# Linear attention beside a shifted MLP on one core: half rows of w4 in three openings, another order of the first products, one straight program

## The chip, the cores and the metric

The kernel runs on 1 core of one Trainium2 chip. The metric is device time in microseconds (us). Below, PE is TensorE (matrix products), DVE is VectorE, ACT is ScalarE, POOL is GpSimd and SP is SyncE, which issues most transfers. PSUM is the memory that PE writes to: 8 banks, each 512 float32 wide on 128 partitions.

## What is computed

```python
def reference(A_x, A_wqkv, A_wo, B_x, B_w1, B_w2, B_w3, B_w4, gate_w):
    x = A_x                                              # (1, 2048, 640)
    g = sigmoid((x * gate_w).sum(-1, keepdims=True))
    # a: linear attention, 32 heads of 20
    q, k, v = heads(x @ wqkv)
    phi = lambda t: where(t > 0, t + 1, exp(t)) + 1e-6
    kv = einsum("bhsd,bhse->bhde", phi(k), v)
    z = einsum("bhsd->bhd", phi(k))
    a = (phi(q) @ kv / (phi(q) . z + 1e-6)) @ wo
    # b: two gelu layers with layer norms, the first one's columns shifted by 1 or 2 rows
    h = gelu(layernorm(x) @ w1)                          # (640, 640)
    x1 = x + shifted(h) @ w2
    b = x1 + gelu(layernorm(x1) @ w3) @ w4               # (640, 1728), (1728, 640)
    return g * a + (1 - g) * b
```

Inputs and output are bfloat16; sums are float32 in PSUM.

## The kernel before

The 2048 rows are 16 tiles of 128, or 4 chunks of 512. A product over 640 columns of depth is 5 blocks of 128 (`KD`), one over 1728 is 13 blocks of 128 (`KFF`) and a half block of 64.

**Order.** The program is written as items (`_Items.add`) in streams, each with dependencies. A planner (`_Items.run`, line 352) takes the next item of the stream that can start first by a simulated clock, and the engines' programs are lists in that order. `_Sched.op` derives each instruction's waits from what it reads and writes. A lag of `None` in a dependency means order alone. `bank()` and `pair()` give out PSUM banks, the one that comes free first by that clock; `bank_hold` keeps banks out of their reach.

**Emission.** `_Sched.emit` (line 300) opens an `nc.Block()`, writes each engine's list as a body of its own in it, and adds final waits: POOL waits for every transfer in, SP for every transfer out, in the order of their last use.

**First stage.** `t_x` turns a tile of x by PE (five 128 x 128 products against an identity) and DVE copies it to `xT`. `q_four` (line 916) makes queries of tiles 0 to 3 with `stream` (line 893): a step (t, k) of its list is a 512 and a 128 column product with block k of `wq`; (t, None) is `t_x(t)`. Tile 0 is turned ahead of the list. `k_first` (line 925) makes keys of tile 0 the same way with `wkg`, 512 and 130 columns: the last two are a column of ones and the gate's weights, which have a transfer of their own. `phi` then reads the pair of banks with ACT and DVE. Tiles 1 to 3 are `k_tile`; from tile 4 on, the x tile is turned by a transfer on SP ("trx") and query and key tiles alternate. Between them stand the G steps (`gr_step`), which sum keys times x over all tiles, a 512 and a 128 column product each, in a pair of banks held through the whole stage; G steps 0, 1 and 2 stand behind key tile 4.

**Last stage.** `w3_group` (c, j) makes 128 of the 1728 hidden columns for chunk c into `h2T`, which has two slots. `w3_half` makes the last 64 columns for two chunks at once into `h2h`: an even tile's rows on partitions 0 to 63, an odd tile's on 64 to 127. w4's products for a tile t take columns 128 to 640 (`w4_tile`, 13 products that end in DVE's sum into `x_tok`); columns 0 to 128 are made for a whole chunk turned (`w4_turned`, then ACT's copy and a transposing transfer to `tl`, then `turned_sum` by DVE, 9 operations). The half block of 64 has only half of the array's height. `w4_half(c)` (line 1193) makes these products for a whole chunk first, opening 5 banks that the 13 full products add to later: one turned product with partitions 64 to 127 (`first`), four mains, alternately low and high, and one turned product with partitions 0 to 63. `w4_tile` of tile 15 is cut in 384 and 128 columns, so the last chunk takes 6 banks. `w4_half(0)` stands behind `w3_half(2)`, ahead of `w3_group(1, 11)`; the other three ahead of `w4_turned(c)`. Attention tiles (`a_tile`, five products of 512, and `a_turned` for a chunk) come between w4's tiles, and `out_tiles` sends finished tiles.

Of the kernel before, what the change touches and what calls it, by code (L numbers as in the profile page):

```python
# [51 lines left out]
class _Sched:  # L52
# [247 lines left out]
    def emit(self):  # L300
        nc = self.nc
        with ExitStack() as es:
# [5 lines left out]
            for k, n in self.dma_cnt.items():  # L308
                if not k.startswith("out"):
                    self.prog["pool"].append(([("d:" + k, 16 * n)], None, None))  # L310
            last = {k: i for i, k in enumerate(self.out_order)}
            for k in sorted(last, key=last.get):
                self.prog["sp"].append(([("d:" + k, 16 * self.dma_cnt[k])], None, None))
            block = es.enter_context(nc.Block())
            engs = {"pe": ("tensor", block.tensor), "act": ("scalar", block.scalar), "dve": ("vector", block.vector),
                    "pool": ("gpsimd", block.gpsimd), "sp": ("sync", block.sync)}

            def body(name):
                prog = self.prog[name]

                def run(e):
                    for (waits, fn, sem) in prog:
                        for (sk, val) in waits:
                            e.wait_ge(sems[sk], val)
                        if fn is None:
                            continue
                        ins = fn(e)
                        if sem is not None:
                            if sem.startswith("d:"):
                                ins.then_inc(sems[sem], 16)  # L330
                            else:
                                ins.then_inc(sems[sem], 1)
                return run

            for name, (_, deco) in engs.items():
                if self.prog[name]:
                    deco(body(name))
# [95 lines left out]
def _build(nc, A_x, A_wqkv, A_wo, B_w1, B_w2, B_w3, B_w4, gate_w, out, dbg=None, stop=None):  # L433
# [491 lines left out]
    def k_first():  # L925
        stream([(0, k) for k in range(KD)], wkg, 130, k_out)
# [11 lines left out]
    for i in range(4, NT + 2):  # L938
        if i < NT:
# [4 lines left out]
        for t in range(3) if i == 4 else (i - 2,):  # L944
# [465 lines left out]
```

## Time and profile before

| | us |
|---|---|
| median of 3 runs | 261.06 (260.98 to 261.1) |
| the profiled execution | 261.21 |
| its span | 259.1 |
| PE busy | 254.9 |
| DVE busy | 158.4 |
| ACT busy | 110.8 |
| POOL busy | 97.3 |

The span is the time from the first to the last instruction of one profiled execution; the metric is a little longer. A row of a timeline has start and duration in us, engine, line of the kernel, operation, out<-in, shape and count, and in brackets how long the engine had been idle and what ended that. Neighbouring instructions of one kind are merged in one row. A row of groups has the count, the busy time and the mean in ns. A row of waits has the sum in us, how many, and the longest. A row of transfers has the count, the size, and the median time from issue to landing. The granted PE clock is full in all 40 slices.

### The profile page before, as it was taken

What the parts mean: (1) busy time and instruction counts of PE and PEld (TensorE: products, weight loads), DVE (VectorE), ACT (ScalarE), POOL (GpSimd) and SP (SyncE); (2) the same over time, 40 slices, a digit from 0 to 9 for tenths busy, and PEclk for the clock granted to TensorE, in tenths of its full rate; (3) what the DMA queues carried; (4) which work ended last, traced back from release to release, by engine and by line L of the source; (5) the groups of instructions that cost most, each with busy time, mean ns of one, the idle gap of its engine ahead of it and who ended that gap; (6) DMA issues with size and microseconds to landing.
All of it is one profiled execution on the core that took longest, in us unless ns stands there. A gap on an engine that the chain in (4) does not pass through costs nothing.

```text
span 259.1 us, 3851 instructions
## 1 busy us (share of the span) xinstructions
PE 254.9 (98%) x1427; PEld 121.8 (47%) x1427; DVE 158.4 (61%) x293; ACT 110.8 (43%) x229; POOL 97.3 (38%) x154
## 2 busy tenths in 40 slices
PE   7999999999999999999999999999999999999996
PEld 3555555544445455554444444444444444444443
DVE  2497877899954699989995303998006510048136
ACT  1496777741355857684864240015510055200100
POOL 8003996869944119659681210111002210003000
PEclk9999999999999999999999999999999999999999
DMA  6858997826528699483677513115110040010322
GB/s 196 260 79 232 180 119 191 237 49 125 101 45 108 114 374 330 86 100 65 127 122 111 108 20 23 25 25 145 28 23 0 1 123 0 0 20 0 92 53 101
DMA packets 58644, 26.78 MB, mean 103 GB/s; under 512 B 49966, under 2 KB 57215, under 8 KB 58626
## 3 DMA queue, kind: packets, MB, share of 16 engines
q1 hardware_dynamic: 57122, 22.92, 42.5%
q0 software_dynamic: 1168, 3.28, 5.3%
q10 hardware_dynamic: 336, 0.35, 0.4%
q8 instruction: 11, 0.18, 0.3%
q14 instruction: 7, 0.06, 0.1%
HBM read 12.09 MB, written 2.67 MB: 57 GB/s over the span
## 4 chain that ended last, share of the span: by engine, by line
PE 97%; DMA 1%; DVE 0%; SPq 0%; issue 0%
PE ps L622 61%; PE ps L1227 22%; PE ps L828 7%; PE ps L909 2%; DMA x_tok<-in_A_x_dram 1%; PE ps L808 1%; PE ps L1127 1%; PE ps L1205 1%; PE ps L910 0%; PE ps L991 0%; PE ps L1210 0%; PE ps L809 0%; SPq L289 0%; PE ps L633 0%; PE ps L1024 0%; DVE xT L687 0%
## 5 line engine op out<-in xcount | busy, mean ns | idle before, releaser
L622 PE MATMUL ps<-xnT,w 128*128 128x512 bf16 x360 | 81.5, 379 | 0.0
L622 PEld LDWEIGHTS ps<-xnT,w 128*128 128x128 bf16 x360 | 34.5, 98 | 39.3 <-issue 0.2
L661 DVE SCALAR_TENSOR_TENSOR x_tok<-ps,stg,abx 128x512 bf16<-128x512 f32 (+2 forms) x17 | 12.2, 717 | 60.3 <-PE ps L1227 60.2
L1227 PE MATMUL ps<-w,h2T 128*128 128x512 bf16 (+2 forms) x221 | 47.0, 366 | 0.0
L644 POOL TENSOR_SCALAR abx<-x_tok,stg 128x512 f32<-128x512 bf16 x16 | 12.4, 779 | 92.1 <-DVE x_tok L661 71.6
L644 POOL TENSOR_SCALAR xn<-x_tok,st 128x640 bf16<-128x640 bf16 x32 | 38.7, 1218 | 8.9 <-DMA xnT<-xn 8.5
L678 ACT ACTIVATE h2T<-ps 128x512 bf16<-128x512 f32 x52 | 29.9, 600 | 23.5 <-PE ps L622 23.5
L1227 PEld LDWEIGHTS ps<-w,h2T 128*128 128x128 bf16 x221 | 21.2, 98 | 24.1
L678 ACT ACTIVATE tlT<-ps 128x512 bf16<-128x512 f32 x8 | 4.8, 597 | 60.7 <-PE ps L622 49.6
L678 ACT ACTIVATE Er<-ps 128x640 bf16<-128x640 f32 (+1 forms) x35 | 22.9, 660 | 18.2 <-PE ps L622 9.7
L677 ACT ACTIVATE junk<-x_tok 128x640 bf16<-128x640 bf16 x32 | 23.6, 738 | 4.7 <-DVE x_tok L659 4.2
L678 ACT ACTIVATE hsT<-ps 128x512 bf16<-128x512 f32 (+1 forms) x32 | 18.9, 595 | 14.1 <-PE ps L622 13.8
L622 PE MATMUL ps<-w,hsT 128*128 128x512 bf16 (+1 forms) x160 | 24.0, 299 | 0.0
L622 PE MATMUL ps<-wkg,xT 128*128 128x512 bf16 (+1 forms) x150 | 22.6, 299 | 0.0
L622 PE MATMUL ps<-M_sb,pqnT 128*128 128x512 bf16 x80 | 19.7, 379 | 0.0
L622 PEld LDWEIGHTS ps<-w,hsT 128*128 128x128 bf16 x160 | 13.4, 98 | 12.5
L622 PEld LDWEIGHTS ps<-wkg,xT 128*128 128x128 bf16 x150 | 12.6, 97 | 11.8
L828 PE MATMUL ps<-pk_tok,x_tok 128*128 128x512 bf16 x80 | 17.8, 379 | 0.0
L659 DVE SCALAR_TENSOR_TENSOR x_tok<-ps,x_tok 128x640 bf16<-128x640 f32 x16 | 13.1, 821 | 7.5 <-PE ps L622 6.9
L661 DVE SCALAR_TENSOR_TENSOR abx<-ps,stg,abx 128x512 f32<-128x512 f32 x16 | 11.9, 748 | 9.1 <-PE ps L622 6.4
L652 DVE TENSOR_TENSOR qprod<-qprod,pk_tok 128x640 f32<-128x640 f32 x13 | 16.3, 1254 | 0.4
L644 DVE TENSOR_SCALAR Er<-Er 128x640 bf16<-128x640 bf16 (+1 forms) x35 | 11.6, 332 | 8.0 <-ACT Er L678 7.0
(87 smaller groups left out, 284.5 us busy)
## 6 DMA issues: line engine op xcount, KB each, us to landing
w<-in_B_w_dram SPq DMA_DIRECT2D x1, 2160.0 KB, 10.0
w<-in_B_w_dram SPq DMA_DIRECT2D x1, 2080.0 KB, 15.5
x_tok<-in_A_x_dram SPq DMA_DIRECT2D x3, 640.0 KB, 6.0
out_dram<-x_tok SPq DMA_DIRECT2D x3, 640.0 KB, 3.4
w<-in_B_w_dram POOLq DMA_DIRECT2D x8, 160.0 KB, 5.1
wkg<-in_A_wqkv_dram SPq DMA_DIRECT2D x5, 160.0 KB, 4.3
wv<-in_A_wqkv_dram POOLq DMA_DIRECT2D x1, 800.0 KB, 5.8
x_tok<-in_A_x_dram SPq DMA_DIRECT2D x4, 160.0 KB, 3.4
```

The source lines that it names most:

```text
L622: ins = e.matmul(out_ap, l, r, start=(i == 0), stop=(i == n - 1))
L644: return engf(lambda e: e.tensor_scalar(out_ap, in_ap, s1, s2, op0, op1), rd, [out_ap], cost=cost)
L652: return engf(lambda e: e.tensor_tensor(out_ap, a, b_, op), [a, b_], [out_ap], cost=cost)
L659: return dve(lambda e: e.scalar_tensor_tensor(out_ap, in0, scalar, in1, op0, op1, accum_out=accum), rd, [out_ap, accum], cost=cost + 70.0)
L661: return dve(lambda e: e.scalar_tensor_tensor(out_ap, in0, scalar, in1, op0, op1), rd, [out_ap], cost=cost)
L677: return act(lambda e: e.activation(out_ap, in_ap, func, bias=bias, scale=scale, accum_out=accum), rd, wr, cost=cost)
L678: return act(lambda e: e.activation(out_ap, in_ap, func, bias=bias, scale=scale), rd, wr, cost=cost)
L808: e.matmul(ps[:, b, :], l, x_tok[:, t, 0:512], start=(t == 0), stop=(t == NT - 1))
L828: ins = e.matmul(ps[:, b, :], l, r, start=(t0 + q_ == 0), stop=(t0 + q_ == NT - 1))
L909: e.matmul(ps[:, b, 0:512], l, w[:, k, 0:512], start=(k == 0), stop=(k == KD - 1))
L1127: ins = e.matmul(o, l, r, start=st, stop=sp)
L1227: ins = e.matmul(o, l, r, start=False, stop=(i == KFF - 1), skip_group_check=shared)
```

## The change

Four things are changed. The program is emitted straight on the engines, without a block, with a barrier at its end; POOL's final waits are gone, and SP waits for the outputs in reverse order and for those transfers in that nobody waits for. `q_four`'s order is another, `k_first` makes its five wide products first, and G steps 0 and 1 stand ahead of query tile 4. `w4_half` becomes `w4_enter`: three lists of seven units (c, i), where i = 4 is a chunk's turned bank. Entry 0 stands behind both `w3_half`, which now come after `w3_group(1, 12)`; entry 1 behind w4's tile 5; entry 2 behind tile 11 and the last `a_turned`. With that the turned products and the sums move: `w4_turned(1)` behind tile 5, `w4_turned(3)` behind tile 12, and `turned_sum` 0 to 3 behind tiles 1, 6, 12 and 13.

```diff
@@ -305,36 +305,20 @@
                 sems["c:" + e] = es.enter_context(nc.semaphore("cnt_" + e))
             for k in self.dma_cnt:
                 sems["d:" + k] = es.enter_context(nc.semaphore("dma_" + k))
-            for k, n in self.dma_cnt.items():
-                if not k.startswith("out"):
-                    self.prog["pool"].append(([("d:" + k, 16 * n)], None, None))
+            seen = {w for p in self.prog.values() for (waits, _fn, _sem) in p for w in waits}
             last = {k: i for i, k in enumerate(self.out_order)}
-            for k in sorted(last, key=last.get):
+            left = [k for k in self.dma_cnt if k not in last and ("d:" + k, 16 * self.dma_cnt[k]) not in seen]
+            for k in sorted(last, key=last.get, reverse=True) + left:
                 self.prog["sp"].append(([("d:" + k, 16 * self.dma_cnt[k])], None, None))
-            block = es.enter_context(nc.Block())
...
+            engs = {"pe": nc.tensor, "act": nc.scalar, "dve": nc.vector, "pool": nc.gpsimd, "sp": nc.sync}
+
+            for name, e in engs.items():
+                for (waits, fn, sem) in self.prog[name]:
+                    for (sk, val) in waits:
+                        e.wait_ge(sems[sk], val)
+                    if fn is not None:
+                        fn(e).then_inc(sems[sem], 16 if sem.startswith("d:") else 1)
+            nc.all_engine_barrier()
 
 
 class _Items:
@@ -914,8 +898,8 @@
                 done(t, b)
 
     def q_four():
-        order = [(0, 0), (1, None), (2, None), (1, 0), (2, 0), (0, 1), (1, 1), (2, 1), (3, None), (0, 2), (1, 2), (3, 0), (0, 3), (1, 3),
-                 (0, 4), (2, 2), (1, 4), (2, 3), (2, 4), (3, 1), (3, 2), (3, 3), (3, 4)]
+        order = [(0, 0), (1, None), (2, None), (1, 0), (0, 1), (1, 1), (2, 0), (2, 1), (3, None), (0, 2), (1, 2), (0, 3), (0, 4), (1, 3),
+                 (1, 4), (2, 2), (2, 3), (2, 4), (3, 0), (3, 1), (3, 2), (3, 3), (3, 4)]
         stream(order, wq, 128, lambda t, b: phi(b, pq_tok[:, t + 1, :]))
 
     def k_out(t, b):
@@ -923,7 +907,13 @@
         activation(junk[:, 0, :], x_tok[:, t, :], ACTF.Square, accum=st1[:, 1, t:t + 1])
 
     def k_first():
-        stream([(0, k) for k in range(KD)], wkg, 130, k_out)
+        b = pair()
+        for c0, c1, b_ in ((0, 512, b), (512, D + 2, b + 1)):
+            for k in range(KD):
+                l, r, o = xT[:, k, 0:128], wkg[:, k, c0:c1], ps[:, b_, 0:c1 - c0]
+                pe(lambda e, l=l, r=r, o=o, k=k: e.matmul(o, l, r, start=(k == 0), stop=(k == KD - 1)), [l, r], [o],
+                   cost=(c1 - c0) * 0.4167 + 2.5)
+        k_out(0, b)
 
     def addA(name, dur, fn, deps=()):
         IT.add("A", name, dur, fn, deps)
@@ -936,12 +926,15 @@
     for i in range(1, 4):
         addA(("k", i), 1.36, lambda t=i: k_tile(t))
     for i in range(4, NT + 2):
+        if i == 4:
+            for t in range(2):
+                addA(("g0", t), 0.27, lambda t=t: gr_step(t), deps=[(("k", t), 2.0)])
         if i < NT:
             addA(("q", i), 1.08, lambda t=i: q_tile(t))
             addA(("k", i), 1.36, lambda t=i: k_tile(t))
             if i % 4 == 3:
                 addA(("qr", i // 4), 1.08, lambda c=i // 4: q_turned(c))
-        for t in range(3) if i == 4 else (i - 2,):
+        for t in (i - 2,):
             addA(("g0", t), 0.27, lambda t=t: gr_step(t), deps=[(("k", t), 2.0)])
 
     IT.add("LW", ("lw1",), 0.0, load_w1, deps=[(("k", 5), 0.0)])
@@ -1190,35 +1183,48 @@
     def w4_cuts(t):
         return ((0, 384), (384, 512)) if t == NT - 1 else ((0, 512),)
 
-    def w4_half(c):
-        tag_chk("h2T", c % 2, c)
-        bs = [bank() for _ in range(5 if c < NCH - 1 else 6)]
-        w4_banks[c] = bs
-        bank_hold.update(bs)
-        mains = []
-        for i in range(4):
-            for n, (n0, n1) in enumerate(w4_cuts(4 * c + i)):
-                mains.append((ps[:, bs[i if n == 0 else 5], 0:n1 - n0], i, 128 + n0, 128 + n1))
-
-        def main(e, o, i, n0, n1):
+    ENTRIES = (((0, 4), (0, 0), (0, 1), (0, 2), (0, 3), (1, 0), (1, 1)),
+               ((1, 4), (1, 2), (1, 3), (2, 0), (2, 1), (2, 2), (2, 3)),
+               ((2, 4), (3, 4), (3, 0), (3, 1), (3, 2), (3, 3)))
+
+    def w4_enter(units):
+        mains, heads, tails = [], [], []
+        for n_, (c, i) in enumerate(units):
+            if i == 4:
+                b = bank()
+                w4_banks[c, 4] = [b]
+                bank_hold.add(b)
+                heads.append((c, b, 1 if n_ == 0 else 0))
+                tails.append((c, b, 0 if n_ == 0 else 1))
+                continue
+            tag_chk("h2T", c % 2, c) if c == units[0][0] else None
+            bs = w4_banks[c, i] = [bank() for _ in w4_cuts(4 * c + i)]
+            bank_hold.update(bs)
+            for b, (n0, n1) in zip(bs, w4_cuts(4 * c + i)):
+                mains.append((ps[:, b, 0:n1 - n0], c, i, 128 + n0, 128 + n1))
+
+        def main(e, o, c, i, n0, n1):
             rows = slice(64 * (i % 2), 64 * (i % 2) + 64)
             return e.matmul(o, h2h[rows, c, 128 * (i // 2):128 * (i // 2 + 1)], w4[rows, KFF, n0:n1], start=True, stop=False)
 
-        def turned(e, par):
+        def turned(e, c, b, par, first):
             rows = slice(64 * par, 64 * par + 64)
-            o = ps[:, bs[4], :].rearrange("p (n h q) -> p n h q", h=2, q=128)[:, :, par, :]
+            o = ps[:, b, :].rearrange("p (n h q) -> p n h q", h=2, q=128)[:, :, par, :]
             return e.matmul(o, w4[rows, KFF, 0:128], h2h[rows, c, :].rearrange("p (n q) -> p n q", q=128),
-                            start=(par == 1), stop=False, skip_group_check=True)
+                            start=first, stop=False, skip_group_check=True)
 
         def fn(e):
             ins = None
             for m in mains:
                 ins = main(e, *m)
             return ins
-        rd = [h2h[:, c, :], w4[:, KFF, :]]
-        first = pe(lambda e: turned(e, 1), rd, [ps[:, bs[4], :]], cost=60.0)
-        pe(fn, rd, [m[0] for m in mains], cost=540.0)
-        pe(lambda e: turned(e, 0), rd, [ps[:, bs[4], :]], cost=110.0, after=first)
+
+        def rd(cs):
+            return [h2h[:, c, :] for c in sorted(set(cs))] + [w4[:, KFF, :]]
+        done = [pe(lambda e, h=h: turned(e, *h, True), rd([h[0]]), [ps[:, h[1], :]], cost=60.0) for h in heads]
+        pe(fn, rd([m[1] for m in mains]), [m[0] for m in mains], cost=len(mains) * 110.0)
+        for f, h in zip(done, tails):
+            pe(lambda e, h=h: turned(e, *h, False), rd([h[0]]), [ps[:, h[1], :]], cost=110.0, after=f)
 
...
@@ -1262,9 +1268,10 @@
 
     def w3_w4_half():
         w3_half(2)
-        w4_half(0)
+        w4_enter(ENTRIES[0])
 
     GEL = 1.3
+    TS_AT = {1: 0, 6: 1, 12: 2, 13: 3}
     OUT_AT = {3: 0, 7: 4, 11: 8, 13: 12, 14: 14, 15: 15}
     for c in range(NCH):
         for j in range(KD):
@@ -1312,10 +1319,10 @@
                 deps.append((("w2", NT - 1), 0.0))
             if c == 1 and 7 <= j <= 10:
                 deps.append((("a", j - 7), 0.0))
-            if c == 1 and j == KFF - 2:
+            IT.add("W3", ("w3", c, j), 1.08, lambda c=c, j=j: w3_group(c, j), deps)
+            if c == 1 and j == KFF - 1:
                 IT.add("W3", ("w3h", 0), 1.27, lambda: w3_half(0), [(("t2", u), 0.9) for u in range(4, 8)])
-                IT.add("W3", ("w3h", 2), 2.03, w3_w4_half, [(("t2", u), 0.9) for u in range(12, 16)] + [(("a", 3), 0.0), (("w4load",), 0.0)])
-            IT.add("W3", ("w3", c, j), 1.08, lambda c=c, j=j: w3_group(c, j), deps)
+                IT.add("W3", ("w3h", 2), 2.03, w3_w4_half, [(("t2", u), 0.9) for u in range(12, 16)] + [(("a", 3), 0.0), (("at", 0), 0.0), (("w4load",), 0.0)])
     for t in range(NT):
         deps = [(("zb",), 1.0), (("qr", max(t // 4, 1)), 2.0)]
         if t < 7:
@@ -1342,21 +1349,23 @@
         IT.add("AT", ("a", t), 1.08, lambda t=t: a_tile(t), deps)
         if t % 4 == 3:
             IT.add("AT", ("at", c), 1.08, lambda c=c: a_turned(c), [(("qt", t), 3.0)] + ([(("ts", c - 2), 0.0)] if c >= 2 else []))
-        deps4 = [(("a", t), 0.0), (("w3h", c - c % 2), GEL), (("w3", c, KFF - 1), GEL)]
-        if t % 4 == 0:
-            deps4.append((("w3", min(c + 1, NCH - 1), KFF - 1), 0.0))
-            if t == 0:
-                deps4.append((("a", 3), 0.0))
-                deps4.append((("w3h", 2), 0.0))
-        elif t + 3 < NT:
+        deps4 = [(("a", t), 0.0), (("w3h", 2), GEL), (("w3", c, KFF - 1), GEL), (("w3", min(c + 1, NCH - 1), KFF - 1), 0.0)]
+        if t % 4 != 0 and t + 3 < NT:
             deps4.append((("a", t + 3), 0.0))
-        if t % 4 == 0:
-            if c > 0:
-                IT.add("W4", ("w4h", c), 0.76, lambda c=c: w4_half(c), deps=deps4)
-            IT.add("W4", ("w4t", c), 2.8, lambda c=c: w4_turned(c), deps=deps4 + [(("at", c), 0.0)])
+        if t == 14:
+            deps4.append((("ts", 3), None))
+        if t == 6:
+            IT.add("W4", ("w4h", 1), 0.95, lambda: w4_enter(ENTRIES[1]), deps=deps4)
+            IT.add("W4", ("w4t", 1), 2.8, lambda: w4_turned(1), deps=[(("at", 1), 0.0)])
+        if t == 12:
+            IT.add("W4", ("w4h", 2), 0.95, lambda: w4_enter(ENTRIES[2]), deps=[(("at", 2), 0.0), (("at", 3), 0.0)])
+            IT.add("W4", ("w4t", 2), 2.8, lambda: w4_turned(2))
+        if t == 0 or t == 13:
+            IT.add("W4", ("w4t", c), 2.8, lambda c=c: w4_turned(c), deps=deps4 + [(("at", c), 0.0)] + ([(("ts", 2), None)] if c == 3 else []))
         IT.add("W4", ("w4", t), 2.8, lambda t=t: w4_tile(t), deps=deps4)
-        if t % 4 == 1:
-            IT.add("TS", ("ts", c), 0.0, lambda c=c: turned_sum(c), deps=[(("w4", t), None), (("w4t", c), 4.0), (("at", c), 4.0)])
+        if t in TS_AT:
+            u = TS_AT[t]
+            IT.add("TS", ("ts", u), 0.0, lambda u=u: turned_sum(u), deps=[(("w4", t), None), (("w4t", u), 4.0), (("at", u), 4.0)])
         if t in OUT_AT:
             IT.add("OUT", ("out", t), 0.0, lambda t=t: out_tiles(OUT_AT[t], t + 1), deps=[(("w4", t), 0.0), (("ts", c), 0.0)])
 
```

More of the change, by code (lines that the diff above doesn't have):

```diff
@@ L1232, in w4_turned @@
         tag_chk("h2T", c % 2, c)
-        b = w4_banks[c][4]
+        b = w4_banks[c, 4][0]
         w4_acc(ps[:, b, :], [(w4[:, k, 0:128], h2T[:, c % 2, k, :]) for k in range(KFF)], True)
@@ L1243, in w4_tile @@
         for n, (n0, n1) in enumerate(w4_cuts(t)):
-            b = w4_banks[c][a if n == 0 else 5]
+            b = w4_banks[c, a][n]
             o = ps[:, b, 0:n1 - n0]
```

20 lines of the change are left out of this document (removed).

## The prediction

> **What bounds the kernel now.** I read the share of busy time by engine first, then the view of what TensorE (PE) waited for, then the timeline of the stretches that the change touches.
>
> ```profile
> PE 254.9 (98%) x1427; PEld 121.8 (47%) x1427; DVE 158.4 (61%) x293; ACT 110.8 (43%) x229; POOL 97.3 (38%) x154
> ...
> PE ps L877 <- PEq L1395: 0.8, 1, 0.8
> PE ps L633 <- DMA x_tok<-in_A_x_dram: 0.5, 2, 0.3
> PE ps L909 <- DVE xT L687: 0.3, 1, 0.3
> ```
>
> PE is busy for 98% of the span, and the three rows are all the waits that the view of its waits has for the whole execution; the last two lie in the first 7 us. After that PE is an unbroken queue of products. So time is won only by waits in the head, by products that cost more than their columns, and by what lies behind the last product; what the other engines do counts only where it opens a gap.
>
> **The head: order of the first query products, K tile 0, two early G steps.**
>
> ```profile
> 5.41 0.45 PE L633 MATMUL ps<-ident,x_tok 128*128 128x128 bf16 x5 [0.32 <-DMA x_tok<-in_A_x_dram]
> 5.70 0.38 PE L909 MATMUL ps<-wq,xT 128*128 128x512 bf16 x1
> 5.90 0.49 DVE L687 COPY xT<-ps 128x640 bf16<-128x640 bf16 x1 [0.28 <-PE ps L633]
> 6.45 0.39 PE L909 MATMUL ps<-wq,xT 128*128 128x512 bf16 x1 [0.32 <-DVE xT L687]
> 6.73 0.38 PE L909 MATMUL ps<-wq,xT 128*128 128x512 bf16 x1
> ...
> 8.86 0.38 PE L909 MATMUL ps<-wq,xT 128*128 128x512 bf16 x1
> ...
> 11.57 0.38 PE L909 MATMUL ps<-wq,xT 128*128 128x512 bf16 x1
> ```
> ```profile
> 2.18 0.43 SPq L289 DMA_DIRECT2D wq<-in_A_wqkv_dram  x1
> 4.56 2.33 SPq L289 DMA_DIRECT2D wkg<-in_A_wqkv_dram  x5
> 6.93 0.43 SPq L288 DMA_DIRECT2D wkg<-in_gate_w_dram  x1
> 13.54 6.24 SPq L285 DMA_TRANSPOSE xT<-x_tok  x4
> ```
> ```profile
> wq<-in_A_wqkv_dram SPq DMA_DIRECT2D x1, 160.0 KB, 4.0
> ...
> wkg<-in_A_wqkv_dram SPq DMA_DIRECT2D x5, 160.0 KB, 4.3
> ...
> wkg<-in_gate_w_dram SPq DMA_DIRECT2D x1, 1.2 KB, 5.0
> ...
> xT<-x_tok SPq DMA_TRANSPOSE x1, 3.4
> ```
>
> The second fence is the issue of transfers on SP (start, duration), the third the time from issue to landing, the fourth number. A step (t, k) of `q_four` is a 512 and a 128 column product; from 8.86 to 11.57 lie ten steps, so one is 0.271 us. Step (2, 0), at 6.45, waits for the copy of tile 2 (5.90 + 0.49 = 6.39). The new order has (0, 1) and (1, 1) there. They need wq's block 1: issued 2.18, landed 2.18 + 4.0 = 6.18, so with the 0.06 from copy to start just seen, (0, 1) starts at 6.24. Four steps to 7.32, five transposes of tile 3 (0.29, as 5.41 to 5.70) to 7.61, fourteen steps without a wait (its tile 3 now comes last, so that its copy is hidden) to 7.61 + 14 x 0.271 = 11.40. Before, the last step ends at 11.57 + 0.27 = 11.84. Gain so far 0.44.
>
> ```profile
> 10.97 0.82 DVE L661 SCALAR_TENSOR_TENSOR pq_tok<-ps,Er 128x640 bf16<-128x640 f32 x1
> 12.02 0.38 PE L909 MATMUL ps<-wkg,xT 128*128 128x512 bf16 x1
> 13.38 4.25 PE L622 MATMUL ps<-wkg,xT 128*128 128x512 bf16 x30
> 16.43 0.82 DVE L661 SCALAR_TENSOR_TENSOR pk_tok<-ps,Er 128x640 bf16<-128x640 f32 x1
> 17.47 1.24 PE L622 MATMUL ps<-wq,xT 128*128 128x512 bf16 x5
> ```
>
> K tile 0 begins at 12.02, not 11.84: each of its steps reads 642 columns of `wkg`, the gate column too, which lands at 6.93 + 5.0 = 11.93. After the change the wide products read 512 columns only; the last block of `wkg` is issued at about 6.46 (five issues in 2.33) and lands near 10.8. So they can follow at 11.40, and the narrow ones come 1.08 later, past the gate's landing. The banks must be free too: the first pair is read until 10.97 + 0.82 = 11.79 now. Tile 0's last step moves from 9.40 (two steps behind 8.86) to 8.42 (four steps from 7.61 on), so that reading ends near 10.8. Gain 0.62 in all. The ten products of the tile are the same; wide first costs nothing by itself.
>
> K tiles 1 to 3 take 17.47 - 13.38 = 4.09, so they end at 12.76 + 4.09 = 16.85. Query tile 4 needs a transposed tile of x, on SP's own schedule: 13.54 + 3.4 = 16.94. That would eat 0.15 of the gain; the two G steps that now stand first fill it: 512 and 128 columns each, 0.54 together, to 17.39. They need `pk_tok` of tile 1, ready at 16.43 + 0.82 = 17.25 before, wanted at 17.12. VectorE's (DVE) chain runs at one tile per (16.43 - 10.97) / 5 = 1.09 and starts 0.98 sooner, so it is there near 16.3. Query tile 4 starts 0.08 sooner with 0.54 of later work done: **0.62** stays. If DVE's chain did not move, the second step would wait 0.2 and 0.42 would be left; if later transfers take it back, 0. Both ends stay for the range. Opening G's pair of banks earlier leaves three pairs for queries and keys, as later in the loop.
>
> **The half rows: three excursions for four.**
>
> ```profile
> 186.50 1.03 PE L622 MATMUL ps<-xnT,w 128*128 128x512 bf16 x4
> 187.46 0.28 PE L1210 MATMUL ps<-h2h,w 64*128 64x256 bf16 x1
> 187.46 0.71 PE L1205 MATMUL ps<-w,h2h 64*128 64x512 bf16 x4
> ...
> 188.10 0.82 PE L1227 MATMUL ps<-h2T,w 128*128 128x512 bf16 x3
> ```
>
> One record of a 512-column product is 0.38 long, products overlap: four in 1.03 start every (1.03 - 0.38) / 3 = 0.217. The last one starts at 187.15, the next full-height product was due at 187.37 and starts at 188.10: an excursion takes 0.73. Inside, half-height products start every (0.71 - 0.38) / 3 = 0.11, two at a time in the two halves of the array. Four of them and two of half that length are 0.55; 0.18 is lost in going and coming back. Four excursions are 2.92. The new three carry the same 25 products: twice six mains, 0.73 + 0.22 = 0.95, and once four with two more turned products, 0.73 + 0.11 = 0.84; 2.74 in all. Gain **0.18**, from 0 (if the wait to come back is longer with more banks open) to 0.25.
>
> Each entry now takes seven of eight banks, so the bank that was read last but one must be free.
>
> ```profile
> 150.12 0.60 ACT L678 ACTIVATE h2h<-ps 128x512 bf16<-128x512 f32 x1 [0.61 <-PE ps L1127]
> ...
> 240.87 0.75 DVE L661 SCALAR_TENSOR_TENSOR x_tok<-ps,stg,abx 128x512 bf16<-128x512 f32 x1 [1.37 <-PE ps L1227]
> 241.84 0.28 PE L1210 MATMUL ps<-h2h,w 64*128 64x256 bf16 x1
> ```
>
> Entry 0 comes right behind the two half-row products of w3 as before, only these now stand behind the last group of chunk 1. Its data and the seventh bank come from one reading, 150.12 to 150.72, and the excursion starts at 151.1 since the second half-row group hides it (0.4 to spare; 0.6 if that cover were gone). Entries 1 and 2 come behind an attention group of five products (1.08), as the fourth does now: w4's tile is read from 240.87 to 241.62, the entry starts at 241.84, 0.2 later. The eighth bank, which the attention group has just filled, is the one left out. Cost 0. Here the rule speaks against the change: the Trainium skill, TensorEngine Tiling (Array Packing), Gotcha 1: PSUM Pressure, says that row tiling raises the pressure on PSUM, with its row tiles in different banks; no row above shows a wait from it, and by it the entries would wait, which is the second rival.
>
> **The end.**
>
> ```profile
> 257.14 0.34 SPq L289 DMA_DIRECT2D out_dram<-x_tok  x1
> ...
> out_dram<-x_tok SPq DMA_DIRECT2D x1, 32.0 KB, 1.5
> ...
> SPq L302 <- PEq L302: 0.2, 1, 0.2
> ```
>
> The last transfer lands at 257.14 + 1.5 = 258.64; the span ends at 259.1, 0.46 later, with SP's other final waits, its jump and the barrier in it. The jump goes, and by waiting for the last transfer first SP finds the others done. The row of SP's exit bounds the gain at 0.2; 0 if the barrier is all of it; I take the middle, **0.1**. POOL's final waits for input transfers, which go too, were for transfers that products had used long before; they cost nothing. The Trainium skill, Advanced Engine Details and Errata, Control Flow Timing, gives about 108 ns for a compare and branch; by it alone this term would be 0.11, an estimate that no row here isolates.
>
> **Sum.** 0.62 + 0.18 + 0.10 = 0.90. The profiled execution took 261.21, so it becomes 260.31; it lies 0.15 above the median of the runs shown, 261.06, against which the forecast is 260.15.
>
> **The rivals.** (1) *The head's gain is taken back by a transfer on its own schedule.* For: SP issues x and its transposes regardless of PE. Against: PE waits for nothing behind 7 us, and the later transposes belong to tiles that PE reaches many us later. Then 260.15 + 0.62 = 260.77. (2) *The entries wait for a bank.* If DVE reads w4's tile 0.5 later, behind some other work, the 0.2 to spare becomes a wait of 0.3 at entries 1 and 2: 260.75. Against: the sums of the turned columns, DVE's longest stretches there (3.3, next fence), stand behind tiles 1, 6, 12 and 13, none right ahead of an entry.
>
> (3) *The other side: the last sum of the turned columns comes late.*
>
> ```profile
> 246.12 1.20 SPq L285 DMA_TRANSPOSE tl<-tlT  x1
> 251.78 0.68 DVE L652 TENSOR_TENSOR tlu<-tl,x_tok 128x512 f32<-128x512 bf16 x1
> 255.09 0.75 DVE L661 SCALAR_TENSOR_TENSOR x_tok<-ps,stg,abx 128x512 bf16<-128x512 f32 x1
> 256.03 1.08 DVE L661 SCALAR_TENSOR_TENSOR x_tok<-ps,stg,abx 128x384 bf16<-128x384 f32 x2 [0.19 <-PE ps L1227]
> tl<-tlT SPq DMA_TRANSPOSE x1, 2.4
> ...
> out_dram<-x_tok SPq DMA_DIRECT2D x3, 640.0 KB, 3.4
> ```
>
> Its transpose, issued 246.12, lands at 248.5, and the sum starts at 251.78: 3.3 to spare. The change puts w4's tile 12 ahead of that product, 13 x 0.217 = 2.8, and leaves 0.5. The sum lasts till 255.09, and DVE then idles 0.19 before its last tiles. So from 0.7 of lateness on, the end moves one for one. Counted from the end of chunk 2's turned product, tile 12's products end at 2.8, its reading about 0.9 later, the sum of chunk 2 at 2.8 + 0.9 + 3.3 = 7.0; only then can SP send the 640 KB of tiles 8 to 11. Chunk 3's turned product ends at 5.6, its copy takes 0.8 with the way to it, so its transpose can go at 6.4. Where SP has the output first in its queue, the transpose goes at 7.0 + 0.6 = 7.6, 1.2 late, and the end moves by 0.5; where it then waits out that transfer too, 3.4 more. Middle 2: 262.15, slower. For it: the margin shrinks to a sixth. Against: the planner issues work by when it can start, and the turned product can start at 2.8, the output at 7.0.
>
> **Chances.** Forecast 0.72, rival 1 0.08, rival 2 0.08, rival 3 0.06, and 0.06 that the planner's order elsewhere shifts and opens a gap of some tenths or more. This measurement tells about 0.2%, 0.5 us, from nothing. Faster by more: the forecast, and 0.08 from rivals 1 and 2 where they take only part: 0.80. Within: 0.11. Slower: 0.09. The range goes from all upper bounds (0.65 + 0.25 + 0.2 + a tenth of scatter: 259.85) to rivals 1 and 2: 259.85 to 260.8.
>
> **What would show it.** Right: (0, 1) near 6.24, K tile 0 near 11.4, query tile 4 near 17.4 behind two G steps, PE's view still without waits behind 7 us; three groups of half-height products, none opened by a wait on DVE; DVE's reading of the last tile, at 256.03 now, near 255.2; span near 258.2. Wrong: a releaser named ahead of the half-height products, a gap in PE between 17 and 150, the last sum of turned columns starting later than 5 us before PE's end, or more than 0.5 between the last landing and the end.

## The result, and the profile after

| | before | after |
|---|---|---|
| median of 22 runs each, one chip, us | 261.07 (260.58 to 261.58) | 260.06 (259.54 to 262.09) |
| ratio, with its 95% interval | | 0.9964 (0.9956 to 0.9972) |
| profiled execution, us | 261.21 | 260.06 |
| its span, us | 259.11 | 258.33 |
| time beyond the span, us | 2.10 | 1.73 |

The change makes the kernel 0.36% faster, about 1.0 us: more than the 0.2% that can be told. The forecast of 260.15 is 0.09 off. The table already holds something that the forecast did not have: 0.37 of the 1.15 between the two profiled executions lies outside the span.

The share of busy time, and all of what TensorE (PE) waited for, of the kernel after:

```profile
PE 254.8 (99%) x1427; PEld 122.7 (47%) x1427; DVE 158.2 (61%) x293; ACT 110.9 (43%) x229; POOL 96.8 (37%) x154
...
PE ps L861 <- PEq L1404: 0.8, 1, 0.8
PE ps L893 <- DVE xT L671: 0.3, 1, 0.3
PE ps L617 <- DMA x_tok<-in_A_x_dram: 0.2, 1, 0.2
```

As many products as before, and as before no wait behind 7 us in this view. The view has a limit: the record of a product is longer than the step to the next one, so short waits hide in it. The 0.18 that key tile 0 waited in the profile of before (11.84 to 12.02, by the prediction's own reading) is not among that kernel's waits. The starts of the products have to tell such waits. PE's busy time fell by only 0.1, although the span fell by 0.8: the sum of busy time would not have found this gain. The head, from PE's timeline:

```profile
3.77 0.71 PE L617 MATMUL ps<-ident,x_tok 128*128 128x128 bf16 x5 [0.23 <-DMA x_tok<-in_A_x_dram]
...
6.21 0.39 PE L893 MATMUL ps<-wq,xT 128*128 128x512 bf16 x1 [0.31 <-DVE xT L671]
...
6.49 0.38 PE L893 MATMUL ps<-wq,xT 128*128 128x512 bf16 x1
...
11.61 0.22 PE L894 MATMUL ps<-wq,xT 128*128 128x128 bf16 x1
11.66 1.53 PE L914 MATMUL ps<-wkg,xT 128*128 128x512 bf16 x10
...
17.11 0.38 PE L792 MATMUL ps<-x_tok,pk_tok 128*128 128x512 bf16 x1
...
17.66 1.24 PE L606 MATMUL ps<-wq,xT 128*128 128x512 bf16 x5
...
20.37 1.24 PE L606 MATMUL ps<-wq,xT 128*128 128x512 bf16 x5
```

The same view of before, query tile 5, which stands behind the same products in both kernels (queries, keys, G steps 0 to 2):

```profile
20.73 1.24 PE L622 MATMUL ps<-wq,xT 128*128 128x512 bf16 x5
```

The order is the forecast one: (1, 0) at 6.21, then (0, 1), K tile 0 right behind the last query step, two G steps, query tile 4 with no wait. Yet tile 5 comes only 0.36 sooner, and every time stands 0.25 behind the forecast: (0, 1) at 6.49 for 6.24, K tile 0 at 11.66 for 11.40, query tile 4 at 17.66 for 17.4. The first row says where it was lost. Five products of 128 columns take 0.71 here; in the profile of before the same kind took 0.45. Up to about 5.4 us PE works at half pace, and step (1, 0) is late before the new order has begun.

The three excursions, from PE's timeline:

```profile
152.89 0.92 PE L1208 MATMUL ps<-w,h2h 64*128 64x512 bf16 x6
...
193.91 1.24 PE L606 MATMUL ps<-M_sb,pqnT 128*128 128x512 bf16 x5
195.08 0.28 PE L1213 MATMUL ps<-h2h,w 64*128 64x256 bf16 x1
...
195.95 0.82 PE L1233 MATMUL ps<-h2T,w 128*128 128x512 bf16 x3
...
237.18 1.24 PE L606 MATMUL ps<-pqnT,M_sb 128*128 128x512 bf16 x5
238.36 0.28 PE L1213 MATMUL ps<-h2h,w 64*128 64x256 bf16 x2
238.48 0.59 PE L1208 MATMUL ps<-w,h2h 64*128 64x512 bf16 x5
...
239.11 0.82 PE L1233 MATMUL ps<-h2T,w 128*128 128x512 bf16 x3
```

No row names a releaser. The first, at 152.89, has its six mains right behind the half rows of w3. The second: five products from 193.91 on start every 0.215, so the next full-height product was due at 194.99; it starts at 195.95, an excursion of 0.96. The third by the same reckoning: 238.26 to 239.11, 0.85. The forecast had 0.95, 0.95 and 0.84. DVE's (VectorE's) readings that free the seventh bank:

```profile
194.11 0.75 DVE L645 SCALAR_TENSOR_TENSOR x_tok<-ps,stg,abx 128x512 bf16<-128x512 f32 x1 [1.49 <-PE ps L1233]
...
237.38 0.75 DVE L645 SCALAR_TENSOR_TENSOR x_tok<-ps,stg,abx 128x512 bf16<-128x512 f32 x1 [2.05 <-PE ps L1233]
```

They end at 194.86 and 238.13, each 0.2 before its entry, as the forecast had it. The last transfers on SP (SyncE), and DVE's last work:

```profile
248.36 1.19 SPq L285 DMA_TRANSPOSE tl<-tlT  x1
249.60 6.05 SPq L289 DMA_DIRECT2D out_dram<-x_tok  x3
...
256.57 0.34 SPq L289 DMA_DIRECT2D out_dram<-x_tok  x1
```
```profile
251.22 0.68 DVE L636 TENSOR_TENSOR tlu<-tl,x_tok 128x512 f32<-128x512 bf16 x1
...
254.53 0.74 DVE L645 SCALAR_TENSOR_TENSOR x_tok<-ps,stg,abx 128x512 bf16<-128x512 f32 x1
255.47 1.08 DVE L645 SCALAR_TENSOR_TENSOR x_tok<-ps,stg,abx 128x384 bf16<-128x384 f32 x2 [0.19 <-PE ps L1233]
```

The last transpose goes ahead of the outputs in SP's queue. With the 2.4 that it takes to land (its row, as in before) it is there at 250.76, 0.46 before the sum of the turned columns. DVE still idles 0.19 before its last two readings, so the sum does not set the end. The last output is issued at 256.57 and, with its 1.5, lands at 258.07; the span ends 0.26 later, where before it was 0.46. (At the trace's full resolution 0.29 and 0.49; below I use these.)

DVE's last reading comes at 255.47 for 256.03, 0.56 sooner: the head's 0.36 and 0.20 of the excursions, with nothing taken back between. One of the forecast's signs of being wrong was badly set: the last sum of turned columns starting later than 5 us before PE's end. It starts 4.93 before it (PE's timeline of after, then of before), but with 251.78 of before it is 4.94 there too.

```profile
247.54 8.61 PE L1233 MATMUL ps<-w,h2T 128*128 128x512 bf16 x52
```
```profile
245.30 11.42 PE L1227 MATMUL ps<-w,h2T 128*128 128x512 bf16 x65
```

So the gain of the two profiles is 0.36 in the head, 0.20 in the excursions, 0.20 at the end, and 0.37 outside the span. The head's is little more than half of its forecast, and the last was in none. The experiments ask what each part is worth by itself, why the head shows so little, and what shortens the time outside the span.

### The profile page after: what moved, and what is told of

It reads as the page before. It is cut to its first block, busy times and chain, and to the rows that moved or that the text cites. A ratio compares the mean times of both kernels' runs of the same rounds, so it can differ in the third digit from the quotient of the medians.

```text
span 258.3 us, 3824 instructions
## 1 busy us (share of the span) xinstructions
PE 254.8 (99%) x1427; PEld 122.7 (47%) x1427; DVE 158.2 (61%) x293; ACT 110.9 (43%) x229; POOL 96.8 (37%) x154
## 4 chain that ended last, share of the span: by engine, by line
PE 97%; DMA 1%; DVE 0%; issue 0%
PE ps L606 61%; PE ps L1233 22%; PE ps L812 7%; PE ps L893 2%; PE ps L792 1%; DMA x_tok<-in_A_x_dram 1%; PE ps L1120 1%; PE ps L1208 1%; PE ps L617 1%; PE ps L914 1%; PE ps L894 0%; PE ps L984 0%; PE ps L793 0%; PE ps L1213 0%; PE ps L1017 0%; DVE xT L671 0%
```

## The experiments

All kernels do the whole computation. The unchanged kernel ran beside each of the four groups, and medians and ratios are against that.

### One part at a time

The first run has the emission alone (both hunks of `emit`, with the new final waits), the second `q_four`, `k_first` and the G steps alone, the third the half rows alone; the fourth is the kernel before, unchanged. Their edits are the hunks of the diff:

```diff
-            block = es.enter_context(nc.Block())
...
+            engs = {"pe": nc.tensor, "act": nc.scalar, "dve": nc.vector, "pool": nc.gpsimd, "sp": nc.sync}
...
+            nc.all_engine_barrier()
```

> The kernel before with the new emission alone. Theory A (the prediction's sum): only the end of the span changes, 0.1 us; the time falls by 0.1, within what can be told. Theory B (two profiles: 0.46 of the span lay behind the last landing before and 0.25 after; the time less the span was 2.1 before and 1.76 after): the straight program saves about 0.2 at the end of the span and 0.35 outside it, 0.5 to 0.6 in all, and the products start and run as before.

```diff
-        stream([(0, k) for k in range(KD)], wkg, 130, k_out)
+        b = pair()
+        for c0, c1, b_ in ((0, 512, b), (512, D + 2, b + 1)):
...
+        if i == 4:
+            for t in range(2):
+                addA(("g0", t), 0.27, lambda t=t: gr_step(t), deps=[(("k", t), 2.0)])
```

> The kernel before with the head's three edits alone. Theory A: 0.62 us less. Theory B (in the changed kernel's profile the products between 3.8 and 5.4 us ran at half pace, and key tile 0 began at 11.66, not 11.40): 0.36 less whenever PE comes to full pace late, 0.6 when it comes early; so 0.35 to 0.6, and the start of the first full-pace product differs from run to run. Time less span stays 2.1 by both.

```diff
-    def w4_half(c):
...
+    def w4_enter(units):
...
-        w4_half(0)
+        w4_enter(ENTRIES[0])
```

> The kernel before with the half-row edits alone. Theory A: 0.18 us less; three groups of half-height products, 0.95, 0.95 and 0.84 long, none opened by a wait. Theory B (rival 2 of the prediction, banks): no gain or a loss, with a gap ahead of an entry that the profile names DVE for. Time less span stays 2.1 by both.

The unchanged kernel:

> The kernel before, unchanged, as a measure of what a run of it scatters in its parts: ratio 1.000 by every theory; time less span 2.1 in every run if that belongs to its program; the moment at which PE's first products reach full pace differs from its first profile if that pace depends on the run and not on the program.

Measured, against 261.13 (33 runs of the kernel before):

| kernel | median, us (11 runs) | ratio, 95% |
|---|---|---|
| emission alone | 260.93 | 0.9989 (0.998 to 0.9998) |
| head alone | 260.71 | 0.9981 (0.9973 to 0.999) |
| half rows alone | 261.04 | 0.9995 (0.9986 to 1.0003) |
| unchanged | 261.32 | 1.0005 (0.9996 to 1.0014) |

The three single gains add up to 0.35%; the whole change has 0.36%. With intervals of about 0.09% to either side, that shows only that the parts neither help nor hinder each other much. The emission alone was expected at 0.1 by the prediction's sum and at 0.5 to 0.6 by its rival; 0.11% is 0.3, between them. The half rows alone are too little for the times to tell, and the profile has to tell them. PE's timeline and DVE's last row, first of the unchanged kernel, then of the half rows alone:

```profile
77.45 1.13 PE L991 MATMUL ps<-GT,wv 128*64 128x60 bf16 x55
...
256.37 1.08 DVE L661 SCALAR_TENSOR_TENSOR x_tok<-ps,stg,abx 128x384 bf16<-128x384 f32 x2 [0.20 <-PE ps L1227]
```
```profile
77.43 1.13 PE L991 MATMUL ps<-GT,wv 128*64 128x60 bf16 x55
...
256.15 1.08 DVE L661 SCALAR_TENSOR_TENSOR x_tok<-ps,stg,abx 128x384 bf16<-128x384 f32 x2 [0.19 <-PE ps L1240]
```

From the same product in the middle to the last reading it is 178.92 unchanged and 178.72 with the half rows alone: 0.20, and the forecast was 0.18. The same stretch, at the trace's full resolution, is 178.92 in all eight profiles of this study with the old half rows and 178.71 or 178.72 in all six with the new, so one pair is enough here.

The unchanged kernel also shows what was wrong with the head. It is the same program as before, and yet its head is later. PE's timeline of this second profile of the kernel before, and then of the head alone:

```profile
3.82 0.71 PE L633 MATMUL ps<-ident,x_tok 128*128 128x128 bf16 x5 [0.27 <-DMA x_tok<-in_A_x_dram]
...
6.33 0.46 PE L909 MATMUL ps<-wq,xT 128*128 128x512 bf16 x1
6.62 0.22 PE L910 MATMUL ps<-wq,xT 128*128 128x128 bf16 x1
...
21.07 1.24 PE L622 MATMUL ps<-wq,xT 128*128 128x512 bf16 x5
```
```profile
3.77 0.72 PE L633 MATMUL ps<-ident,x_tok 128*128 128x128 bf16 x5 [0.22 <-DMA x_tok<-in_A_x_dram]
...
6.59 0.22 PE L910 MATMUL ps<-wq,xT 128*128 128x128 bf16 x1
...
20.53 1.24 PE L622 MATMUL ps<-wq,xT 128*128 128x512 bf16 x5
```

Here half pace lasts till 6.6 in both. Query tile 5 comes at 21.07 and at 20.53: 0.54 sooner. The profile of before that the forecast was made from had its full pace by 3.74 us; that of after only at 5.5. Comparing those two profiles therefore mixes the change with the pace.

### The head's three edits, one after another

The new order of `q_four` alone, and the order together with the wide products first, the G steps at their old place:

```diff
-        order = [(0, 0), (1, None), (2, None), (1, 0), (2, 0), (0, 1), (1, 1), (2, 1), (3, None), (0, 2), (1, 2), (3, 0), (0, 3), (1, 3),
-                 (0, 4), (2, 2), (1, 4), (2, 3), (2, 4), (3, 1), (3, 2), (3, 3), (3, 4)]
+        order = [(0, 0), (1, None), (2, None), (1, 0), (0, 1), (1, 1), (2, 0), (2, 1), (3, None), (0, 2), (1, 2), (0, 3), (0, 4), (1, 3),
+                 (1, 4), (2, 2), (2, 3), (2, 4), (3, 0), (3, 1), (3, 2), (3, 3), (3, 4)]
```

> The kernel before with the new order of the query products alone. Theory A (the gate column holds key tile 0, 0.18 of the head's 0.62): the queries end 0.3 to 0.45 sooner than in the kernel before at the same pace of PE, but key tile 0 still starts when the gate's transfer has landed, 11.5 to 11.95 us, with a wait in front of it; 0.1 to 0.45 gained. Theory B (the gate is not what holds it): it starts right behind the queries, with no gap, and the gain is that of the head alone, 0.5.

```diff
-        stream([(0, k) for k in range(KD)], wkg, 130, k_out)
+        b = pair()
...
+        k_out(0, b)
```

> The kernel before with the new order and the wide products of key tile 0 first, but the G steps where they were. Theory A (early G steps fill a wait for the turned x tile): query tile 4 starts with a wait when key tile 3 ends ahead of that landing, and the gain is 0.1 to 0.15 less than the head's. Theory B: the tile has landed by then (15.9 in the changed kernel's profile, 16.9 in the one before, against an end of key tile 3 at 17.1), the G steps' place costs nothing, and the gain is the head's, 0.5.

Against 261.18 (31 runs), the order alone took 261.11, ratio 1.0002 (0.9985 to 1.0018); order and wide products 260.81, 0.9984 (0.9974 to 0.9994). The first is inconclusive by its time: its runs lie between 260.36 and 262.86. PE's timeline of it, with the transfer of the gate's column (issued 6.95 on SP, the fourth number is the way to its landing):

```profile
11.63 0.22 PE L910 MATMUL ps<-wq,xT 128*128 128x128 bf16 x1
11.69 0.38 PE L909 MATMUL ps<-wkg,xT 128*128 128x512 bf16 x1
```
```profile
6.95 0.43 SPq L288 DMA_DIRECT2D wkg<-in_gate_w_dram  x1
```
```profile
wkg<-in_gate_w_dram SPq DMA_DIRECT2D x1, 1.2 KB, 4.6
```

The gate lands at 11.55, before 11.69: K tile 0 follows the queries without a gap, and the wide products first would have won nothing. PE's timeline of the second kernel, with its gate transfer:

```profile
11.89 1.53 PE L930 MATMUL ps<-wkg,xT 128*128 128x512 bf16 x10
...
17.34 1.24 PE L622 MATMUL ps<-wq,xT 128*128 128x512 bf16 x5
```
```profile
6.93 0.43 SPq L288 DMA_DIRECT2D wkg<-in_gate_w_dram  x1
```
```profile
wkg<-in_gate_w_dram SPq DMA_DIRECT2D x1, 1.2 KB, 5.1
```

Here the gate lands at 12.03 and K tile 0 starts at 11.89: without the wide products first it would have waited 0.14. Full pace begins early in this execution, as the next rows of PE's timeline show, and yet the head gains little:

```profile
3.73 0.45 PE L633 MATMUL ps<-ident,x_tok 128*128 128x128 bf16 x5 [0.18 <-DMA x_tok<-in_A_x_dram]
...
6.71 0.39 PE L909 MATMUL ps<-wq,xT 128*128 128x512 bf16 x1 [0.35 <-DMA wq<-in_A_wqkv_dram]
...
20.59 0.59 PE L622 MATMUL ps<-wq,xT 128*128 128x512 bf16 x2
```

Step (0, 1) waits here for wq's block 1, which landed at 6.66 (at the trace's full resolution; 6.19 in the profile of before, and between 5.67 and 6.66 over the 14 profiles of this study). Query tile 5, at 20.59, is only 0.14 sooner than the 20.73 of before, which had its full pace as early. So that landing moves the head as well as the pace does.

Query tile 4 stands right behind the keys without a wait although no G step fills the place: at the trace's full resolution its transposed tile of x had landed at 16.32, not 16.94. Over the 14 profiles of this study the gate's landing lies between 11.34 and 12.03, that of the transposed tile between 15.85 and 17.9.

Two of the head's three edits are insurance: they win when PE is early or a transfer late, and nothing otherwise. Of the seven profiles with the new order and at least the same dummy products, the gate lands behind the start of key tile 0 in two, by 0.14 and 0.53; early G steps filled a wait, of 0.15, in one of the six profiles that have them (the one with fewer dummy products). How much of the gain the order has by itself stays open: its one profile has the product at L991 (the one in the middle that was used above) at 76.79, 0.55 ahead of the mean of six profiles with the old head (77.34), but its ten runs show no gain, and order and wide products together 0.16%; the two intervals overlap.

### What shortens the end

The emission has two parts: no block, and other final waits. One run has the straight program with the old waits, the other the block with the new waits.

```diff
             for k, n in self.dma_cnt.items():
                 if not k.startswith("out"):
                     self.prog["pool"].append(([("d:" + k, 16 * n)], None, None))
...
-            block = es.enter_context(nc.Block())
+            engs = {"pe": nc.tensor, "act": nc.scalar, "dve": nc.vector, "pool": nc.gpsimd, "sp": nc.sync}
...
+            nc.all_engine_barrier()
```

> The kernel before, emitted straight with a barrier, but with the old final waits of POOL and SP. Theory A (the jumps are what costs): the span ends 0.3 behind the last landing, not 0.5, and time less span is 1.73 in every run, not 1.92 scattered by 0.1. Theory B (the waits are what costs): 0.5 and 1.92 as before.

```diff
-            for k, n in self.dma_cnt.items():
-                if not k.startswith("out"):
-                    self.prog["pool"].append(([("d:" + k, 16 * n)], None, None))
...
-            for k in sorted(last, key=last.get):
+            for k in sorted(last, key=last.get, reverse=True) + left:
                 self.prog["sp"].append(([("d:" + k, 16 * self.dma_cnt[k])], None, None))
...
             block = es.enter_context(nc.Block())
```

> The kernel before in its block, with the new final waits. Theory A (jumps): 0.5 from the last landing to the end of the span, time less span 1.92, as before. Theory B (waits): 0.3 and 1.73, as in the straight program.

Their times, 261.02 (0.9995, 0.9985 to 1.0004) and 261.03 (0.999, 0.9981 to 0.9999), do not tell the two apart. What does is where each loses its time. From the last landing to the end of the span at full resolution, and the mean time outside the span over the runs:

| kernel | last landing to end of span, us | outside the span, us (runs) |
|---|---|---|
| before (33 runs beside the single parts) | 0.49, 0.50 (two profiles) | 1.91 (1.68 to 2.06) |
| emission, whole | 0.29 | 1.755 (1.69 to 1.81) |
| before (31 runs beside the two below) | | 1.94 (1.68 to 2.18) |
| straight, old waits | 0.31 | 1.86 (1.82 to 1.90) |
| block, new waits | 0.43 | 1.735 (1.70 to 1.77) |
| after (22) | 0.29 | 1.73 (1.68 to 1.81) |

Inside the span most of it goes with the block: 0.18 of 0.21. The trace of before has the place: SP's branch at the block's exit starts at 258.70 and SP's next instruction at 258.88, and the straight program has no such branch. (Over the 14 profiles the first column is 0.49 or 0.50 in all six with the old emission, and 0.29 in all six straight ones with SP's new order of waits.) Outside the span most goes with the waits. Neither change alone has both.

One thing of the forecast falls here. It bounded the block's price by a row of SP's waits, 0.2 at the exit. That row is in the profile of after too, under another line, though nothing is left there to jump out of:

```profile
SPq L321 <- PEq L321: 0.2, 1, 0.2
```

The size was right by luck; the row was another thing, a wait for PE's queue; line 321 is the barrier.

Which of the waits is it? The last run has the kernel after with POOL's 45 final waits (the expectation counted 41) put back, and SP's new order kept:

```diff
+            for k, n in self.dma_cnt.items():
+                if not k.startswith("out"):
+                    self.prog["pool"].append(([("d:" + k, 16 * n)], None, None))
             seen = {w for p in self.prog.values() for (waits, _fn, _sem) in p for w in waits}
```

> The changed kernel with POOL's old final waits back (41 transfers in), SP's new order of waits kept. Theory A (POOL's waits are what lengthens the time outside the span): time less span 1.86, as in the straight program with the old waits, not 1.73; the span itself unchanged, 0.29 behind the last landing; the time 0.13 longer than the changed kernel's. Theory B (SP's order of waits is what matters): 1.73 and no difference.

It took 260.31 (6 runs), 0.9969 (0.9957 to 0.9981). Outside the span 1.895 (1.83 to 1.95), with no run in the range of after; from the last landing to the end 0.29, as after. So POOL's (GpSimd's) final waits cost about 0.17, all of it outside the span. The kernel before, beside it, had 1.88; the kernel after was not run in this group, and its 1.73 is from another. Why is open: most of these waits are for transfers that landed long before. The last is for the last transpose of turned columns, which lands at 250.97, and in the trace POOL is through with all of them by 251.17, while PE works till 256.33 and the span ends at 258.52.

### The pace of the first products

If half pace costs the head 0.3, more dummy products ahead of it could bring the full pace sooner. PE fills its wait for the first tile with them (`WARM` columns). One run takes most of them away, another adds some, also in the gaps of the list ((None, None) is 128 columns more). Only dummy products change. The kernel after runs beside them, unchanged.

```diff
-    WARM = 3072
+    WARM = 512
```

> The changed kernel with 512 columns of dummy products at the start in place of 3072, so that PE idles from 1.3 to 3.7 us. Theory B (PE comes to full pace some time after it has been busy for a while, at 3.5 to 6.9 us in the six profiles so far): full pace comes later, 6.5 to 10 us, and the time rises by 0.5 to 1.7. Rival (the late pace is the run's and has nothing to do with what PE did): no change, within 0.2.

```diff
-    WARM = 3072
+    WARM = 3456
...
-        order = [(0, 0), (1, None), (2, None), (1, 0), (0, 1), (1, 1), (2, 0), (2, 1), (3, None), (0, 2), (1, 2), (0, 3), (0, 4), (1, 3),
+        order = [(0, 0), (1, None), (None, None), (None, None), (2, None), (1, 0), (None, None), (None, None), (0, 1), (1, 1), (2, 0), (2, 1), (3, None), (0, 2), (1, 2), (0, 3), (0, 4), (1, 3),
```

> The changed kernel with more dummy products: 384 columns more at the start and four times 128 in the waits for the third x tile and the second block of wq. Theory B (an idle stretch in the head puts off full pace): full pace never later than 7, fewer late runs, the median 0 to 0.3 lower than the changed kernel's. Rival: the dummies stand in the way of the products behind them (each is 0.05 at full pace, 0.11 at half) and it is 0.1 to 0.3 slower.

> The changed kernel, unchanged, beside the two above: about 0.996 of the kernel before; time less span 1.73 in every run.

With fewer, 261.16, against the kernel before of these runs 0.9997 (0.9984 to 1.001); unchanged, 259.99, 0.9953 (0.9941 to 0.9965); with more, 260.24, 0.9965 (0.9953 to 0.9977). Taking them away gives back the whole gain (1.17 by the medians; in its profile the full pace begins at 7.6, and the span is 259.0 for 258.0). Adding some wins nothing in five runs, and in its profile full pace begins only at 6.8. That idea failed. PE's timeline of the unchanged kernel after in this group:

```profile
3.71 0.45 PE L617 MATMUL ps<-ident,x_tok 128*128 128x128 bf16 x5 [0.16 <-DMA x_tok<-in_A_x_dram]
...
6.12 0.39 PE L893 MATMUL ps<-wq,xT 128*128 128x512 bf16 x1
...
11.30 1.53 PE L914 MATMUL ps<-wkg,xT 128*128 128x512 bf16 x10
...
17.30 1.24 PE L606 MATMUL ps<-wq,xT 128*128 128x512 bf16 x5
...
20.01 1.24 PE L606 MATMUL ps<-wq,xT 128*128 128x512 bf16 x5
```

This execution, like that of before which the forecast was made from, has its full pace by 3.71. Now (0, 1) comes at 6.12 (forecast 6.24), K tile 0 at 11.30 (11.40), query tile 4 at 17.30 (17.4). Query tile 5, at 20.01, is 0.72 sooner than the 20.73 of before, at equal pace, for a forecast of 0.62. Step (0, 1) stands 0.04 behind the landing of wq's block 1 (6.08 at the trace's full resolution), which is what the forecast said would hold it.

## Why the prediction was right

**The head, 0.62.** At equal pace 0.72 (early) and 0.54 (late), and the head alone gains 0.19% of 261.13, 0.5, with an interval of 0.26 to 0.70. Over the profiles, that product at L991, behind the whole head, starts at 77.34 in the mean of six with the old head (77.11 to 77.50) and at 76.75 in the mean of four with the new one and the same dummy products (76.39 to 76.93; line numbers differ): 0.60. The term holds on the average. Its split does not hold in every run: the gate's wait and the place of the G steps count in some executions only. One step was wrong without harm to the sum: the duration of the first products and the landing of wq's block 1 were read from one execution as if they were fixed. The spans of before are 259.1 and 259.4, those of after 258.0 and 258.3, early and late pace; with early pace and a late landing 0.14 was left of the gain.

**The half rows, 0.18.** Measured 0.20 from product to last reading, with excursions of 0.96 and 0.85 where both ends are quoted. Rival 2 (a wait for a bank at the entries) is out: the 0.2 to spare is there at both, and excursions as long as forecast leave no room for a hidden wait. Of the pressure on PSUM that the Trainium skill, TensorEngine Tiling (Array Packing), Gotcha 1: PSUM Pressure, speaks of, and that the prediction set beside this rival, no wait shows here with seven of eight banks taken.

**The end, 0.10.** This step failed, by size and in one part by kind. Inside the span it was 0.20, the upper bound, and not for the row that gave the bound. Outside it, "they cost nothing" was said of POOL's final waits; the run that puts them back shows 0.17. Nor were they all for transfers that had long been used: the last transpose of turned columns is among them. The step assumed that what an engine has done some 7 us before the end is free; in the profile nothing contradicts that, since the price lies outside what the profile covers.

**The sum.** The medians of the spans over the runs fell from 259.2 or 259.3 to 258.3, about 0.95; the terms for the span are 0.54 + 0.20 + 0.20 = 0.94. Outside the span another 0.17 to 0.28 (the last between the kernels run beside the dummy products, 1.99 and 1.71). That makes 1.1 to 1.2; the two comparisons of whole kernels gave 1.01 and 1.27. The forecast's 0.90 is below both: it put the end at half of what the span shows, and left out what lies outside it. That it came within 0.09 of the measured time is in part luck: what it had too small or left out comes to about 0.3, and 1.01 is the smaller of the two comparisons; by the other it is 0.37 short.

**The other rivals.** Rival 1 (a transfer takes the head's gain back) is out: PE's view shows no wait behind 7 us, and the gain at 20 us is still there at the end. Rival 3 (the last turned sum late) is out by its condition: the margin shrank to 0.46, as forecast (0.5), but the transpose went ahead of the output in SP's queue.

## What to carry to other kernels

Before a difference of tenths is read from two profiles, see whether PE had the same pace in both heads, and compare stretches that begin behind it; one more profile of the unchanged kernel did that here. The time outside the span belongs to the kernel as well: final waits that were all satisfied 7 us before the end cost 0.17 us in it, and only the whole time shows it. An edit that removes a wait seen in one profile should be priced over the spread of that landing, not at the one gap.

## What was not expected of the hardware

- The full pace of PE began between 3.7 and 7.6 us of the span over 14 profiles, in three of them by 3.74, with the same 3072 columns of dummy products ahead in twelve of them. The rows show it (0.71 or 0.45 for five products of 128 columns); the page's row of the granted clock, where there is one, reads full in every slice. That row misleads: it takes time without a record as full. The trace's records of the granted clock begin at 3.46 in the profile of before, at 3.49, 6.51 and 7.46 in those of `after_again`, `before_again` and `short_warm`, each just ahead of the first full-pace products, and say nothing of the time before; five traces, that of after among them, have no such record. So "full in all 40 slices" holds only from that time on. The Trainium skill, TensorE: Matmul & The Clock Gate, Part 1, says that a free-running window of activity, some 3.4 us long, decides when half clock ends, and that the transition varies by 0.5 us to either side from run to run. The traces agree that it varies and that the early pace is about half; the onsets of the twelve profiles lie over 3 us apart, not 1, and in the one profile with dummy products added the onset was not early.
- The time outside the span scattered more in the kernel before (1.68 to 2.06 over 33 runs) than after (1.68 to 1.81 over 22). With either of the two changes of the emission alone it scattered little as well (1.82 to 1.90 and 1.70 to 1.77 over ten runs each).
